# A gated-recurrence and soft-MoE kernel: the first k loaded as two transfers, and the transfer of u issued later

## The chip, the cores and the metric

The kernel runs on one core of one Trainium2 chip. The metric is the device time of one execution in microseconds (us); lower is better. A core has five engines that run their own instruction queues: TensorE (PE in the profile, its weight loads PEld), VectorE (DVE), ScalarE (ACT), GpSimd (POOL) and SyncE (SP, which here only issues DMA transfers). A transfer is spread over up to 16 DMA engines; each works through its part of the queue of transfers in order, and it is called a ring below.

## The reference, cut to what matters

There are two stages. The first is a linear recurrence over 768 steps for 4 batches and 8 heads with head size 48; `w` (decay) and `u` (bonus for the present step) hold one row of 48 per head. The second routes the 3072 resulting rows of width 384 through a soft mixture of 8 experts with 4 slots each.

```python
for t in range(S):                                  # r, k, v: (4, 8, 768, 48)
    cur = einsum('bhd,bhe->bhde', u[None] * k[:, :, t], v[:, :, t])
    y[:, :, t] = einsum('bhd,bhde->bhe', r[:, :, t], state + cur)
    state = w[None, :, :, None] * state + einsum('bhd,bhe->bhde', k[:, :, t], v[:, :, t])
x = y.transpose(0, 2, 1, 3).reshape(3072, 384)
logits = x @ phi                                    # (3072, 32)
d = softmax(logits, axis=0); slot_input = (d.T @ x).reshape(8, 4, 384)
for e in range(8):
    slot_out[e] = maximum(slot_input[e] @ w1[e], 0) @ w2[e]    # w1: 384x1024, w2: 1024x384
out = softmax(logits, axis=1) @ slot_out
```

## The kernel before, in words

The recurrence is done in chunks of 128 steps. Six chunks make a batch, and they are handled in 12 units of two chunks (three units a batch). `k`, `r` and `v` come in eight loads each, two per batch: load m is batch m // 2, its even m holds a third of the steps (384 KB, 128 partitions of 2 x 384 numbers), its odd m two thirds (768 KB). The middle dimension of 2 is the parity e of the head: partition p holds for some steps and a pair q of heads first the even head, then the odd one. `load_f` (lines 192 to 196) issues one such load as one transfer on SP.

A load is scaled by powers of w (`Sk`, `Sr`: line 427, a multiplication with a table `tabs` or `tabl`; `VC` is the plain copy of v, line 418), turned on TensorE (`Tk`, `Tr`, `Tv`: line 436) and copied out of PSUM (`Ek`, `Er`, `Ev`: line 359 on ACT, 357 on DVE). Then come the products in the chunk (`A`, line 506, masked by `K`, line 511), the state (`U`, `SM`, `SI`, `SE`), the result (`Y`) and, as results come in, the logits and the dispatch softmax of the second stage.

The expert weights, 16 matrices of 384 x 1024 numbers, are fetched by POOL and turned from f32 into bf16 on the way (`W0` to `W15`, lines 783 and 785). They go mostly into the same 14 buffers `raw` that the loads of k, r and v used. `W0` is issued behind a tiny copy (line 781) that waits for the seventh k. When the last weights are there, the last products (`Q12`, `Q13`, line 921) and one copy (line 928) give `slot_out`; then 24 tiles of the output are computed (line 949), copied out of PSUM (lines 951 and 953) and written by eight transfers on SP (line 955).

The order of nearly all work is written out by hand in the string `ORDER` (line 9). Each word is a task; tasks are emitted in that order, and so each engine's queue holds its own tasks in that order and works through them strictly. Words beginning with F are filler matmuls (line 861) that keep TensorE busy. An instruction waits only for what it reads, and for buffers.

Around the change the words are these. `Lk0`, `Lr0`, `Lv0` load the first k, r and v, `Lk1` and so on the next. `LU` (line 381) loads u, 4 partitions of 96 numbers, 1.5 KB. `CC` on DVE (line 383) runs `consts_c` (lines 290 to 293): a copy of a permutation out of PSUM and then two small copies, of w and of u, into two tiles `wu` (line 293). `CT` (lines 309 to 311) turns both on TensorE, `CA` on DVE copies the result (line 314), `CU` on POOL multiplies w and u into `ucol` (lines 317 and 318), and `CW` on ACT makes the decay `wT`. `ucol` is first read by `U0`. Ahead of all this the small table `w` is loaded by ACT (line 211).

Transfers that SP and ACT issue count on eight completion semaphores in turn, so the ninth of them waits until the first has landed, the tenth for the second, and so on. The order of issue is w, k0, r0, u, v0, k1, r1, v1, k2, r2, v2, k3, r3, v3, k4, ...: k2 waits for w, k3 for u, r3 for v0, v3 for k1, k4 for r1.

Of the kernel before, what the change touches and what calls it, by code (L numbers as in the profile page):

```python
# [6 lines left out]


ORDER = """
CB0 Lk0 Sk0 Lr0 Tk0 Sr0 LU Lv0 Ek0:ACT VC0:ACT Lk1 AHa AHb F0_2 Tr0 Lr1 PR0 TB0b F1_3 N0 TB0a F2_2 Tv0 Ev0 Lv1 CC Lk2  # L10
TB1b F3a_9 V0 CT Sk1b Sr1b Sk1a:DVE Lr2 Er0:ACT NE0:ACT CA F4a_11 Tk1b F5a_1 Tk1a VE0 A00 CB TB1a Ek1a VC1b VC1a:ACT
Lv2 CU K00 F6_4 Tr1b Tv1a Ek1b:ACT CW Ev1a Lk3 Sr1a F7y_1 U0 Er1b:ACT SM0 Sk2 N2 A01 K01 NE2:ACT Tv1b Sr2 Ev1b:ACT
Sk3a F8y_3 Tr1a SI0 Lr3 Lv3 N1 Sk3b Er1a:ACT Lk4 VC3b PR1b V1 A10 Sr3a DV0 VC2:ACT K10 Y0 NE1:ACT VE1:ACT Sr3b YE0 Tv2
# [32 lines left out]
class _Plan:  # L46
# [7 lines left out]
    def buf(self, pool):  # L54
        return _Buf(pool)

    def add(self, name, engs, fn, deps=(), bufs=()):
        self.by[name] = _Task(name, engs, fn, list(deps), list(bufs))
# [23 lines left out]
def kernel(  # L82
# [13 lines left out]
    B, H, S, D = r.shape  # L96
# [11 lines left out]
    R = 8  # L108
# [5 lines left out]
    CC = NS // U3  # L114
# [11 lines left out]
    def O(ins):  # L126
        return tc.keep_in_program_order(ins)

    pe, dve, act, pool, sp = nc.tensor, nc.vector, nc.scalar, nc.gpsimd, nc.sync
# [5 lines left out]
    RW = 2 * J * D  # L135
# [53 lines left out]

    def load_f(dst, a, m):
        b, lg = divmod(m, 2)
        jn = J if lg else JH
        O(sp.dma_start(out=dst[:, 0:2 * jn * D].rearrange("p (e x) -> p e x", e=2),  # L195
                       in_=a[b].rearrange("h (y j) d -> y h (j d)", j=jn)[lg * CC * R:lg * CC * R + 32]))

# [146 lines left out]
    def consts_d():  # L344
# [5 lines left out]
    L = _Plan(dict(raw=raw, ks=ks_t, vj=vj_t, kn=kn_t, vn=vn_t, AT=AT_t, prs=pr_t[0:1], prl=pr_t[1:2], dv=dv_t,  # L350
                   **{f"{x}T": t for x, t in turned.items()},
                   S=S_t, Z=Z_t, x=x_t, zc=zc_t, Lc=Lc_t, Lcl=[Lc_t[0][:, NS - 2:]], Lsl=[Ls_t[0][:, NS - 2:]], Ls=Ls_t, E=E_t, ET=ET_t, T=T_t, A=[Ab], Y=[Yb], M=[Mb], **{f"xT{j}": [t] for j, t in enumerate(xT_t)}))
    buf, add = L.buf, L.add
# [17 lines left out]
    for m in range(NLD):  # L371
        for i, nm in enumerate("krv"):

            b, o = (kr["k", m][0], RH) if nm == "r" and m % 2 == 0 else (buf("raw"), 0)
            kr[nm, m] = b, o
            add(f"L{nm}{m}", "SP", (lambda b, o, a, m: lambda t: load_f(b.inst[:, o:RW], a, m))(b, o, (k, r, v)[i], m), bufs=[b])

    def load_phi(t):
        O(sp.dma_start(out=phi_f, in_=moe_phi.rearrange("(p q) s -> p q s", q=nM)))
# [13 lines left out]
    for h, av_, x in (("a", argl, slice(0, JH + 1)), ("b", argm, slice(JH, J + 1))):  # L393
        add(f"AH{h}", "DVE", (lambda av_, x: lambda t: argv_part(av_, e17l[:, x]))(av_, x))
        for i in range(2):

            add(f"TB{i}{h}", "ACT", (lambda i, h, av_: lambda t: O(act.activation(  # L397
                out=tabl[i][:, :, JH:J] if h == "b" else tabl[i][:, :, 0:JH],
                in_=av_[:, :, 1 - i:JH + 1 - i], func=AF.Exp, scale=(-1.0, 1.0)[i])))(i, h, av_),
# [3 lines left out]
    for m in range(NLD):  # L403
        lg = m % 2
        pb = TT["p", m] = buf("pr" + "sl"[lg])
        for nm in "krv":
            dstT = TT[nm, m] = buf(nm + "sl"[lg] + "T")
            P = P2 if nm == "v" else 128
            for h in range(1 + lg):
# [11 lines left out]
                else:  # L421
                    i = "kr".index(nm)
# [42 lines left out]
    for n in range(NU):  # L465
# [4 lines left out]
        m = 2 * bt + (ui > 0)  # L470
# [50 lines left out]
        def f_su(t, Mf=Mf, kn=kn, vn=vn, Sold=Sold, pb=pb, n=n, NK=NK):  # L521
# [13 lines left out]
            bufs=[Mf, vn, pb_, kn] + ([Sold] if ui else []))  # L535
# [26 lines left out]
        def f_y(t, Yf=Yf, rT=rT, vn=vn, dvb=dvb, Sold=Sold, Smid=Smid, a=tuple(ATb), n=n):  # L562
# [18 lines left out]
            bufs=[Yf, rTb, vn, dvb, Smid, ATb[0], ATb[1]] + ([Sold] if ui else []))  # L581
# [213 lines left out]
    for n in range(2 * E):  # L795
        wat[n] = buf("raw")
        wat[n].left += 4
        bufs, deps = [wat[n]], []
# [6 lines left out]
    nm = nm_t[(NPC - 1) % 2]  # L805
# [14 lines left out]
        bufs=[SXb])  # L820
# [118 lines left out]
    i = 0  # L939
# [46 lines left out]
```

## Time and profile before

| what | us |
|---|---|
| median of 3 runs | 119.49 |
| their range | 119.38 to 120.67 |
| the profiled execution, its own time | 120.24 |
| its span in the trace | 118.5 |
| outside the span | 1.7 |
| busy: TensorE, weight loads | 98.0, 71.1 |
| busy: VectorE, ScalarE, GpSimd | 94.8, 86.6, 61.0 |

The span runs from the first to the last instruction that the trace shows; the rest of the execution's time lies around it. The page cuts the span into 40 slices of 2.96 us and prints one digit for each: 9 means busy for 90% or more. DMA is the mean busy share of the 16 rings. The chain of waits starts at the last instruction and follows back what released it. All moments below are us from the start of the span. The trace also records when each ring reports its part of a transfer as landed; a transfer has landed when its last ring has reported.

### The profile page before, as it was taken

The page shows a single profiled execution, that of the slowest core. Times are in us where ns is not written, and L with a number is a line of the kernel's source. Part 1 is how long each engine was busy: PE and PEld are TensorE (multiplying, and loading weights), DVE is VectorE, ACT ScalarE, POOL GpSimd, SP SyncE. Part 2 cuts the span into 40 slices and gives each one's busy share as a digit, 9 for nine tenths or more (in the row PEclk, how much of TensorE's full clock was granted, in tenths as well). Part 3 has the DMA queues.
Part 4 walks back from the last instruction along what each step waited for, and adds up shares of the span by engine and source line. Part 5 has one row for each costly group of instructions (what it writes and reads, how often), then busy time and mean ns, then how long its engine had stood idle before and what let it go on. Part 6 is the DMA issues. An engine that isn't in the chain of part 4 may idle for free.

```text
span 118.5 us, 3926 instructions
## 1 busy us (share of the span) xinstructions
PE 98.0 (83%) x1660; PEld 71.1 (60%) x1660; DVE 94.8 (80%) x180; ACT 86.6 (73%) x140; POOL 61.0 (52%) x79
## 2 busy tenths in 40 slices
PE   3997895999999999989999989999899985498000
PEld 0364674787888787867788878686453542254000
DVE  6899987898999999999999989999786274099100
ACT  5769894999999999989899799979644151269000
POOL 7605899999999989999999010002303000000000
PEclk9999999999999999999999999999999999869955
DMA  2999999999999999999999999999999995059994
GB/s 31 333 387 374 364 408 397 383 390 401 384 384 391 297 229 223 219 215 214 217 212 221 210 223 207 223 207 219 212 212 218 216 207 104 12 199 407 419 402 166
DMA packets 10441, 31.81 MB, mean 268 GB/s; under 512 B 1080, under 2 KB 4408, under 8 KB 10424
## 3 DMA queue, kind: packets, MB, share of 16 engines
q0 software_dynamic: 2448, 12.58, 51.8%
q1 hardware_dynamic: 7832, 18.93, 42.3%
q8 instruction: 13, 0.21, 0.7%
q10 hardware_dynamic: 144, 0.05, 0.2%
q14 instruction: 4, 0.03, 0.1%
HBM read 39.42 MB, written 4.72 MB: 373 GB/s over the span
## 4 chain that ended last, share of the span: by engine, by line
PE 32%; DMA 23%; POOL 15%; DVE 9%; ACT 6%; issue 4%; SPq 3%; DVEq 0%; ACTq 0%; POOLq 0%
DMA raw<-in_moe_w_dram 16%; POOL mix L427 12%; PE T L436 7%; DMA raw<-in_r_dram 7%; PE Ab L506 3%; DVE mix L953 2%; PE Yb L572 2%; SPq L195 2%; PE T L491 2%; PE Yb L567 2%; DVE AT_all L511 2%; ACT xT_all L359 2%; PE Yb L578 2%; PE T L481 2%; PE T L595 2%
## 5 line engine op out<-in xcount | busy, mean ns | idle before, releaser
L427 POOL TENSOR_TENSOR mix<-raw,tabl 128x768 bf16<-128x768 f32 x15 | 27.7, 1858 | 5.8 <-ACT tabl L397 5.4
L511 DVE TENSOR_TENSOR AT_all<-Ab,mask 128x1024 bf16<-128x1024 f32 x24 | 29.3, 1219 | 1.1 <-PE Ab L506 0.5
L359 ACT COPY mix<-T 128x1024 bf16<-128x1024 bf16 x19 | 19.1, 1021 | 3.9 <-PE T L436 2.3
L436 PEld LDWEIGHTS <-mix 128*128 128x128 bf16 x192 | 11.8, 99 | 2.3 <-DVE mix L427 0.7
L555 DVE TENSOR_TENSOR dv<-vn,Mb 128x768 bf16<-128x768 bf16 x12 | 11.4, 946 | 1.4 <-PE Mb L545 1.1
L427 POOL TENSOR_TENSOR mix<-raw,tabs 128x768 bf16<-128x768 f32 x6 | 10.8, 1815 | 0.0
L359 ACT COPY vT_all<-T 96x1024 bf16<-96x1024 bf16 x10 | 10.2, 1021 | 0.5 <-PE T L436 0.4
L506 PE MATMUL Ab<-mix 64*128 64x128 bf16 x192 | 9.5, 218 | 1.2 <-ACT mix L359 1.0
L359 ACT COPY xT_all<-T 128x768 bf16<-128x768 bf16 (+1 forms) x12 | 9.3, 784 | 1.3 <-PE T L595 1.3
L359 ACT CAST x<-Yb 128x768 bf16<-128x768 f32 x12 | 9.7, 808 | 0.0
L436 PE MATMUL T<-turnl,mix 128*128 128x128 bf16 x128 | 9.6, 219 | 0.1
L359 ACT COPY vn<-T 128x768 bf16<-128x768 bf16 x11 | 8.8, 814 | 0.0
L452 DVE TENSOR_TENSOR pr<-T,mix 128x1024 bf16<-128x1024 bf16 x12 | 8.0, 681 | 0.0
L712 POOL TENSOR_TENSOR Lc<-Ls,sm 128x192 bf16<-128x192 f32 x2 | 1.0, 516 | 13.5 <-ACT E L690 13.5
L506 PEld LDWEIGHTS <-mix 64*128 64x128 bf16 x192 | 5.8, 94 | 3.5 <-issue 0.7
L572 PEld LDWEIGHTS <-AT_all 128*128 128x128 bf16 x192 | 6.6, 96 | 1.6
L359 ACT COPY kn<-T 128x768 bf16<-128x768 bf16 (+1 forms) x10 | 7.2, 722 | 0.1
L418 POOL CAST vj<-raw 128x768 bf16<-128x768 f32 x8 | 6.7, 832 | 0.6 <-POOL phi_s L336 0.6
L436 PEld LDWEIGHTS <-vj 128*96 128x96 bf16 x96 | 6.2, 123 | 1.2 <-issue 0.2
L572 PE MATMUL Yb<-vn,AT_all 128*128 128x48 bf16 x192 | 6.8, 183 | 0.0
L539 DVE TENSOR_TENSOR Z<-Mb,wT 128x384 bf16<-128x384 f32 x12 | 6.6, 553 | 0.1
L481 PE MATMUL T<-ident,mix 128*128 128x128 bf16 x80 | 6.1, 219 | 0.2
(187 smaller groups left out, 237.8 us busy)
## 6 DMA issues: line engine op xcount, KB each, us to landing
raw<-in_moe_w_dram POOLq DMA_DIRECT2D x13, 768.0 KB, 14.4
raw<-in_k_dram SPq DMA_DIRECT2D x4, 768.0 KB, 12.2
raw<-in_r_dram SPq DMA_DIRECT2D x4, 768.0 KB, 12.2
raw<-in_v_dram SPq DMA_DIRECT2D x4, 768.0 KB, 12.2
out_dram<-mix SPq DMA_DIRECT2D x3, 768.0 KB, 4.6
raw<-in_k_dram SPq DMA_DIRECT2D x4, 384.0 KB, 10.9
raw<-in_r_dram SPq DMA_DIRECT2D x4, 384.0 KB, 10.6
raw<-in_v_dram SPq DMA_DIRECT2D x4, 384.0 KB, 10.8
```

Source lines behind the costliest of these rows:

```text
L195: O(sp.dma_start(out=dst[:, 0:2 * jn * D].rearrange("p (e x) -> p e x", e=2), in_=a[b].rearrange("h (y j) d -> y h (j d)", j=jn)[lg * CC * ...
L359: O(act.copy(dst, src))
L418: O(act.copy(o, i_) if t.eng == "ACT" else pool.tensor_copy(o, i_))
L427: O(eng.tensor_mul(src.inst.rearrange("p (j e s) -> p e j s", j=JH, e=2)[:, :, :, 0:D], rv(), tab))
L436: O(pe.transpose(Tb.inst[0:P, jj * 128:(jj + 1) * 128], sv[:, jj, :], (turn, turnl)[lg][:]))
L452: O(dve.tensor_mul(cv(pb), tv(), cv(kT)))
L481: O(pe.transpose(Tb.inst[:, x * 128:(x + 1) * 128], kT.inst[:, x, :], ident[:]))
L506: O(pe.matmul(Abf.inst[:, e, x * C:(x + 1) * C], kT.inst[s, g * nQ + x, :], rT.inst[s, g * nQ + x, :]))
L511: O(dve.tensor_mul(AT.inst[:], Abf.inst[:].rearrange("p e (g t) -> p e g t", g=nQ), mask[:, None, None, :].to_broadcast([128, 2, nQ, C])))
L539: O(dve.tensor_mul(Smid.inst[:], Mf.inst[:, 0:SW].rearrange("p (q d) -> p q d", q=nQ)[:, :, None, :].to_broadcast([128, nQ, 2, D]), wT[:, ...
L555: O(dve.tensor_mul(dvb.inst[:].rearrange("p g e d -> p (g e) d"), vn.inst[:].rearrange("p g e d -> p (g e) d"), Mf.inst[:, 448:448 + 2 * P ...
L572: O(pe.matmul(y[:, x // nQ, q * P2 + e * D:q * P2 + (e + 1) * D], a[x // nQ].inst[:, e, q, :], vn.inst[:, x, e, :], start=False, stop=(c = ...
```

## The change

The first k is loaded by two transfers, one for the even heads and one for the odd heads, 192 KB each, with the same rows of 1536 bytes. `LU` moves in `ORDER` from its place ahead of `Lv0` to the place behind `Lv1`. All else stays in its order on every engine: on SP the queue becomes k0 even, k0 odd, r0, v0, k1, r1, v1, u, k2, ... Among the eight semaphores the order is now w, k0 even, k0 odd, r0, v0, k1, r1, v1, u, k2, ...: u waits for w, k2 and r2 for the halves of k0, v2 for r0, k3 for v0, r3 for k1, v3 for r1, k4 for v1, r4 for u. `Sk0` waits for both halves.

```diff
 ORDER = """
-CB0 Lk0 Sk0 Lr0 Tk0 Sr0 LU Lv0 Ek0:ACT VC0:ACT Lk1 AHa AHb F0_2 Tr0 Lr1 PR0 TB0b F1_3 N0 TB0a F2_2 Tv0 Ev0 Lv1 CC Lk2
+CB0 Lk0 Sk0 Lr0 Tk0 Sr0 Lv0 Ek0:ACT VC0:ACT Lk1 AHa AHb F0_2 Tr0 Lr1 PR0 TB0b F1_3 N0 TB0a F2_2 Tv0 Ev0 Lv1 LU CC Lk2
...
-    def load_f(dst, a, m):
+    def load_f(dst, a, m, halves=False):
         b, lg = divmod(m, 2)
         jn = J if lg else JH
+        if halves:
+            for e in range(2):
+                O(sp.dma_start(out=dst[:, e * jn * D:(e + 1) * jn * D],
+                               in_=a[b].rearrange("(q e) (y j) d -> e y q (j d)", e=2, j=jn)[e, lg * CC * R:lg * CC * R + 32]))
+            return
         O(sp.dma_start(out=dst[:, 0:2 * jn * D].rearrange("p (e x) -> p e x", e=2),
                        in_=a[b].rearrange("h (y j) d -> y h (j d)", j=jn)[lg * CC * R:lg * CC * R + 32]))
...
-            add(f"L{nm}{m}", "SP", (lambda b, o, a, m: lambda t: load_f(b.inst[:, o:RW], a, m))(b, o, (k, r, v)[i], m), bufs=[b])
+            add(f"L{nm}{m}", "SP", (lambda b, o, a, m, hv: lambda t: load_f(b.inst[:, o:RW], a, m, hv))(b, o, (k, r, v)[i], m, m == 0 and i == 0), bufs=[b])
```

## The prediction

> **What bounds the kernel now.** I read the page's slices first, then the chain of waits, then the stretches and the start in order of time.
>
> ```profile
> span 118.5 us, 3926 instructions
> PEclk9999999999999999999999999999999999869955
> DMA  2999999999999999999999999999999995059994
> ...
> 82.73 18.82 DMA raw<-in_moe_w_dram
> 101.60 0.51 PE Yb L921 x7
> ```
>
> The rings are full from the second slice to the 33rd, then nearly idle for two slices, then full with the output. The chain ends in the last weights, which were issued at 82.73 but landed only at 101.56, because the rings were still working off earlier transfers. So the time is: the rings' start (first packet of k0 at 2.42), their fixed work without a hole, and a tail behind the last weights. In the trace the busy share of the rings stays within a few per cent of full between 3.1 and 97, and the largest dip, between r0 and v0 (4.8 to 5.6), adds up to some 0.1 us. A transfer of weights comes nearest to being late at W7, issued at 60.54, when the first ring runs out of W6 at 64.72: 4.2 us to spare. The engines have slack against this, seen in the next view (busy us of each engine in a stretch, last the granted TensorE clock, DMA share, GB/s).
>
> ```profile
> 10.44:13.85 3.41, 2.29 (x22) 1.35 (x20) 3.30 (x8) 3.41 (x5) 3.07 (x2) 1.00 0.99 353
> 13.85:17.27 3.42, 3.42 (x70) 2.77 (x68) 3.08 (x6) 2.93 (x7) 3.27 (x5) 1.00 1.06 404
> 17.27:20.68 3.41, 2.13 (x36) 1.67 (x34) 2.43 (x4) 1.93 (x3) 3.41 (x3) 1.00 1.03 399
> ...
> 99.20:102.60 3.40, 1.05 (x16) 0.27 (x8) 0.00 (x0) 0.13 (x1) 0.00 (x0) 1.00 0.21 36
> 102.60:106.00 3.40, 3.00 (x11) 1.77 (x11) 2.28 (x5) 2.11 (x5) 0.00 (x0) 0.50 0.32 118
> ```
>
> Between 17.27 and 20.68 PE idles 1.28 and DVE about 1.0, waiting for POOL. Before the last weights PE waits 2.17 (row at 101.60 of the timeline). A lateness of DVE or PE under about 2 us is gone by then. The start, in order of time:
>
> ```profile
> 0.73 0.71 SPq L195 DMA_DIRECT2D raw<-in_k_dram  x1
> 1.49 0.80 SPq L195 DMA_DIRECT2D raw<-in_r_dram  x1
> 2.35 0.53 SPq L381 DMA_DIRECT2D LexpT<-in_u_dram  x1
> 2.91 0.60 SPq L195 DMA_DIRECT2D raw<-in_v_dram  x1
> ...
> 10.68 1.65 DVE L293 COPY wu<-LexpT 4x96 f32<-4x96 f32 x2
> 12.25 0.94 DVE L427 TENSOR_TENSOR mix<-raw,tabl 128x768 bf16<-128x768 f32 x1
> ...
> 12.26 0.34 PE L311 MATMUL Yb<-ident_f,wu 4*128 4x4 f32 x2 [1.12 <-DVE wu L293]
> ```
>
> SP spends 0.5 to 0.8 us on each issue, whatever its size. DVE reaches the copy of u at about 12.1, and PE already waits 1.12 for it.
>
> **The change part by part.**
>
> *k0 in halves.* One issue of 0.71 becomes two. The nearest rows for a half: the first output transfer, also 128 rows of 1536 bytes, took 0.36 to issue, and w on ACT, 128 rows, 0.63. So the second half is issued at 1.1 to 1.4 and done at 1.5 to 2.0. k0's first packet came 0.98 after its issue ended (1.44 to 2.42), so the first half's could come 0.1 to 0.35 sooner. But w's packets share the rings from 2.16 on, and k0's first packets took up to 0.7 us each against 0.065 later; that start-up would not shrink. I take 0.15 sooner; ends 0 and 0.35. The bytes, rows and packets are the same, so the rest of the rings' work keeps its length. k0 as a whole landed at 4.86; DVE began `Sk0` at 5.46, right behind the table that ACT finished at 5.43. So a sooner k0 speeds no engine, and it may be 0.57 later at no cost; after that, DVE's start is late by the same amount. One more semaphore to wait on at `Sk0`: under 0.05, beside ACT's 0.83 on the other table.
>
> *r0* is issued up to 0.6 later (at most 2.0 to 2.8). With k0's 0.98 its packets come at 3.8 at the latest; the fastest ring finished k0 at 3.79, the slowest after 4.4. A hole of 0.0, at most 0.6 if an issue is as slow as r0's 0.80; I take 0. v0, k1, r1 and v1 have one issue more (the half) and one less (u) ahead: 0.3 sooner to 0.1 later. I take 0.05 for the dip at 4.8 to 5.6, where u stood between r0 and v0; ends 0 and 0.1.
>
> *u behind v1.* SP issues u at about 5.6 instead of 2.35, and k2 and all behind it up to 0.6 later: the rings hold k1, r1 and v1 then, until 12.2 at least. The shift in semaphores delays k3, r3, v3 and k4: v3 (issued at 11.30) now waits for r1, landed 12.35, and k4 (12.37) for v1, landed 14.31. The first ring needs k4's packets only at 21.2, when it is done with v3: covered by 6 us. Cost 0.
>
> u itself now lies behind v1 on its rings. Before, it was reported at 5.46 to 5.58 on four rings, amid r0's reports (5.16 to 5.83); the other twelve reports came at once, at 3.00. Now it follows v1, whose rings reported from 12.22 to 14.31, median 12.8. I take 12.9; ends 12.3 and 14.4. The Trainium skill (DMA: Bandwidth & Descriptors, "Why a DMA increments its semaphore by 16") says that a transfer of 4 rows runs on the four lowest engines and that the rest is counted at once; the four late reports agree, but no row says whether the slow ring is among the four.
>
> DVE's copy of u then ends at about 13.0 instead of 12.33. Queued behind it on DVE: `Sk1a`, `CA`, `VE0`, the clearing of Mb, all 0.7 late (0 to 2.1). PE stands at `CT`, and behind it F4a, `Tk1b`, `Tk1a`, the first A. ACT waits for `Tk1b`. POOL wants `wuT` at 15.60 only, and it was there at 13.27: 2.3 to spare. POOL is not late, and PE and DVE regain the 0.7 between 17.27 and 20.68, where they wait for POOL's products. Cost 0 at the end; without that cover 0.7, and 2.17 of waiting before the last weights would still swallow it.
>
> *Sum*: 120.24 of the profiled execution - 0.15 - 0.05 = 120.04. That execution was 0.75 above the median of 119.49, so I forecast **119.3**.
>
> **The rivals.**
>
> *A, the forecast*: rings start slightly sooner, engines hidden: 119.3 (bounds -0.45 to +0: 119.0 to 119.5).
>
> *B, slower: PE falls to half clock behind the late u.* In the stretch before 102.60, PE was busy 1.05 of 3.40, and the next stretch was granted 0.50. With 2.29 and 2.13 of 3.41 the clock stayed. If u lands at 13.5 or later, the stretch 10.44 to 13.85 keeps only about 0.9 (0.51 at 10.63 and the last 0.3). Then 13.85 to 17.27, where PE is full, does half its work: 1.7 late, beside up to 2.1 from the wait. It decides if more than 2.17 of these 3.8 is still there at 99.4: 119.5 + 3.8 - 2.17 = 121.1. For it: PE and DVE are over 95% busy from 30 to 78, and regain little there. Against: the idle 1.28 at 17.3 to 20.7 alone makes it 119.8, and u must be late. The Trainium skill (TensorE: Matmul & The Clock Gate, the rules at its end) puts the limit at idle gaps above about 3 us; by that, a gap from 11.14 to 12.9 costs no clock, and the time would be A's. The trace speaks against so wide a limit: the half clock at 102.60 followed a wait of 2.17.
>
> *C, a hole in the rings behind k0's second half*: r0 comes 0.6 after the rings ran dry, 119.5 + 0.6 - 0.15 = 119.9. Against: the 3.8 and 3.79 above.
>
> *D, faster: the tail keeps its clock.* The output's first matmuls, nine from 103.00 to 105.73, take 2.73 at clock 0.50; at full clock half, 1.36. If the wait before the last weights falls so that no stretch is mostly idle, up to 1.2 of that is saved: 119.3 - 1.2 = 118.1. For it: a shift of the rings' end moves that wait. Against: 0.2 is little, and the copies behind the matmuls (0.49 each on two engines) hide part.
>
> *E, no sooner start*: the start-up packets set the pace, and the halves gain nothing: 119.5. The Trainium skill (DMA: Bandwidth & Descriptors, "Rules for kernel authors") says of two transfers to disjoint partition halves not to bother, since they share the same engines; here it is halves of each row, but by that rule E holds.
>
> **How the numbers follow.** A 0.40, E 0.22, C 0.08, B 0.18, D 0.12. A measurement of this kernel can tell about 1%, 1.2 us, from no change. A, C and E lie within it: same 0.70; B gives slower 0.18, D faster 0.12. The range leaves out half of B and of D with some of the noise of the runs' 1.3: 118.4 to 120.9. The likeliest case's own range is 119.0 to 119.7.
>
> **What would show it.** Two k0 rows on SP of 0.36 to 0.63 each, and v0 issued by 3.0: else the first part is wrong. `Sk0` starting at 5.4 to 5.6. The second copy of L293 ending near 13.0, with PE's wait at L311 near 1.8. POOL's L427 still at 10.3 and 12.5, its ucol near 15.6. Rings full from 3 to 97, last weights at 101.2 to 101.6, a wait of about 2 before them. Wrong would be: a granted 0.50 early on, a PE without a wait before the last weights, a hole in the rings at 3.8.

## The result and the profile after

The changed kernel takes 120.55 us (median of 22 runs, 119.53 to 121.82) beside 119.36 us for the kernel before in the same series (22 runs). The ratio is 1.008, with a 95% interval of 1.0054 to 1.0106: slower, by about 1 us. The profiled execution took 121.15 us with a span of 119.4.

Ratios and intervals here and below leave out runs more than 1.5% above the fastest of their kernel, which takes out six of the twelve runs of e13 (the mean of all twelve is 1.0% above the kernel before) and at most a quarter of the runs of any other variant.

The page of the changed kernel, its slices first. (Lines of the code are six later than before: L427 is L433, L293 is L299, L311 is L317, L921 is L927.)

```profile
span 119.4 us, 3927 instructions
PEclk9999958999999999999999999999999999999965
...
PE 49%; DVE 21%; DMA 7%; issue 5%; ACT 4%; SPq 4%; POOL 2%; DVEq 1%; ACTq 0%
```

Three things are new. The clock is down in the sixth and seventh slice. It is no longer down at the start of the output (before: 8 and 6 in the 35th and 36th). And the chain that ended last holds only 7% of DMA, all of it waiting for u, against 23% before: it ends in PE, not in the last weights. The same stretches as in the prediction (busy us of PE, weight loads, DVE, ACT, POOL; clock; DMA share; GB/s):

```profile
10.44:13.85 3.41, 1.62 (x14) 0.76 (x12) 2.70 (x4) 3.41 (x5) 2.58 (x2) 1.00 1.03 409
13.85:17.27 3.42, 2.31 (x7) 0.89 (x8) 2.54 (x7) 1.86 (x3) 3.27 (x5) 0.69 1.06 386
17.27:20.68 3.41, 3.41 (x44) 2.83 (x43) 1.43 (x2) 1.71 (x5) 1.51 (x1) 0.81 1.03 401
99.20:102.60 3.40, 2.83 (x48) 1.79 (x45) 2.79 (x10) 1.26 (x4) 0.00 (x0) 1.00 0.50 90
102.60:106.00 3.40, 2.79 (x30) 1.82 (x28) 1.69 (x5) 2.00 (x6) 0.00 (x0) 1.00 0.02 5
```

PE did 1.62 us of work between 10.44 and 13.85 where it had done 2.29, and 7 operations in the next stretch where it had done 70. The half clock lies between 15.16 and 18.58. Between 17.27 and 20.68 PE no longer waits for POOL: it is full, and the others wait for it. Between 99.20 and 102.60 PE is busy for 2.83 where it had been for 1.05.

The timeline of the start, SP first, then DVE and PE:

```profile
0.73 1.36 SPq L198 DMA_DIRECT2D raw<-in_k_dram  x2
2.15 0.62 SPq L201 DMA_DIRECT2D raw<-in_r_dram  x1
...
5.68 1.03 SPq L387 DMA_DIRECT2D LexpT<-in_u_dram  x1
```

```profile
5.51 0.96 DVE L433 TENSOR_TENSOR mix<-raw,tabs 128x768 bf16<-128x768 f32 x1
7.28 0.96 DVE L433 TENSOR_TENSOR mix<-raw,tabs 128x768 bf16<-128x768 f32 x1 [0.81 <-DMA raw<-in_r_dram]
...
11.62 1.52 DVE L299 COPY wu<-LexpT 4x96 f32<-4x96 f32 x1
14.61 0.30 DVE L299 COPY wu<-LexpT 4x96 f32<-4x96 f32 x1 [1.46 <-DMA LexpT<-in_u_dram]
```

```profile
14.96 0.22 PE L317 MATMUL Yb<-ident_f,wu 4*128 4x4 f32 x1 [1.54 <-DVE wu L299]
15.11 2.52 PE L867 MATMUL Ab<-mix,ident 128*128 128x512 bf16 x6
...
19.08 0.40 PE L512 MATMUL Ab<-mix 64*128 64x128 bf16 x8
...
101.32 0.83 PE L927 MATMUL Yb<-raw,AT_all 128*32 128x384 bf16 x16 [0.52 <-DVE AT_all L363]
...
103.38 0.50 PE L927 MATMUL Yb<-raw,AT_all 128*32 128x384 bf16 x8
```

The rows of PE before that belong beside them:

```profile
12.53 1.36 PE L861 MATMUL Ab<-mix,ident 128*128 128x512 bf16 x6
...
14.83 0.40 PE L506 MATMUL Ab<-mix 64*128 64x128 bf16 x8
...
101.60 0.84 PE L921 MATMUL Yb<-raw,AT_all 128*32 128x384 bf16 x8 [2.17 <-DMA raw<-in_moe_w_dram]
```

r0 is issued at 2.15 instead of 1.49 and DVE now waits 0.81 for it. u lands only at 14.6, and DVE waits 1.46 for it. PE waits for DVE, and the six filler matmuls behind that wait take 2.52 at the lower clock instead of 1.36. At the end the products of the last weights (103.38) start with no wait at all, where before there was one of 2.17. How the lateness runs through the two traces:

| moment | before | after | later by |
|---|---|---|---|
| DVE starts the first copy into `wu` | 10.68 | 11.62 | 0.94 |
| PE starts the filler behind `CT` | 12.53 | 15.11 | 2.58 |
| PE ends that filler | 13.89 | 17.63 | 3.74 |
| PE starts the first products `A` | 14.83 | 19.08 | 4.25 |
| POOL runs the gate of `W0` | 35.42 | 38.61 | 3.19 |
| PE could start on the last weights (before: 101.60 - 2.17) | 99.43 | 103.38 | 3.95 |
| PE starts on them | 101.60 | 103.38 | 1.78 |
| end of the span | 118.46 | 119.35 | 0.89 |

So in these two executions u holds PE until it is 2.58 late. The 0.94 by which DVE was late because of r0 is no part of a sum here: an earlier DVE would only have waited longer for u. The half clock adds 1.67 by 19.08, where PE has had work without a break. Of these 4.25, PE regains 1.08 by about 22, where it had waited 1.28 for POOL before. Between 47 and 70 it loses 0.97 again, and no run here asks why. Of the 3.95 that are left at the last weights, the former wait swallows 2.17. An output that runs at full clock (0.33 instead of 0.52 for a matmul of 384 columns) goes with 0.89 less behind it.

The rings show the late r0, and more in their bytes than in their busy share. The stretches in which r0 and what follows are fetched, before and then after:

```profile
3.40:4.60 1.20, 1.20 (x5) 0.50 (x4) 0.97 (x3) 0.53 (x3) 1.20 (x3) 1.00 1.02 371
4.60:6.00 1.40, 1.40 (x4) 0.44 (x3) 1.27 (x5) 1.40 (x3) 0.35 (x3) 1.00 1.01 327
6.00:10.00 4.00, 3.88 (x40) 2.53 (x39) 4.00 (x8) 2.65 (x5) 0.00 (x0) 1.00 1.03 389
```

```profile
3.40:4.60 1.20, 1.20 (x5) 0.51 (x4) 0.81 (x2) 0.53 (x3) 1.20 (x3) 1.00 0.93 243
4.60:6.00 1.40, 1.40 (x4) 0.46 (x3) 1.25 (x5) 1.40 (x3) 0.34 (x3) 1.00 0.87 264
6.00:10.00 4.00, 3.70 (x35) 2.37 (x34) 3.19 (x6) 2.11 (x4) 0.00 (x0) 1.00 0.97 315
```

The share falls by a tenth, the bytes by a third (371 to 243 GB/s) and stay a fifth lower until 10. A packet counts as busy as long as it takes, and from 3.6 to 5.3 fourteen packets of 1536 bytes took 0.31 to 1.16 us, where the median of such packets is 0.065 (before, six took 0.35 to 0.53 from 4.0 to 5.8). That these are the first packets behind a pause is likely but not shown: the trace does not tell which ring a packet ran on. By 10 us 2.13 MB of k, r, v and u had come instead of 2.61.

### The profile page after: what moved, and what is told of

Read it like the earlier page. It is cut to its first block, busy times and chain, and to the rows that moved or that the text cites. A ratio compares the mean times of both kernels' runs of the same rounds, so it can differ in the third digit from the quotient of the medians.

```text
span 119.4 us, 3927 instructions
## 1 busy us (share of the span) xinstructions
PE 99.6 (83%) x1660; PEld 72.1 (60%) x1660; DVE 94.4 (79%) x180; ACT 87.0 (73%) x140; POOL 61.3 (51%) x79
## 4 chain that ended last, share of the span: by engine, by line
PE 49%; DVE 21%; DMA 7%; issue 5%; ACT 4%; SPq 4%; POOL 2%; DVEq 1%; ACTq 0%
PE T L442 11%; DMA LexpT<-in_u_dram 7%; DVE AT_all L517 5%; PE Ab L512 4%; DVE mix L959 3%; PE Yb L578 3%; PE Ab L867 3%; SPq L201 3%; PE Yb L927 3%; PE Yb L573 3%; PE Yb L584 2%; PE T L487 2%; PE T L601 2%; PE T L497 2%; PE Mb L535 2%
## 5 line engine op out<-in xcount | busy, mean ns | idle before, releaser
L433 POOL TENSOR_TENSOR mix<-raw,tabl 128x768 bf16<-128x768 f32 x15 | 27.1, 1818 | 6.4 <-ACT tabl L403 6.3
L442 PEld LDWEIGHTS <-mix 128*128 128x128 bf16 x192 | 12.3, 102 | 3.3 <-DVE mix L433 1.7
L433 POOL TENSOR_TENSOR mix<-raw,tabs 128x768 bf16<-128x768 f32 x6 | 10.8, 1820 | 2.3 <-PE Yb L867 2.3
L442 PE MATMUL T<-turnl,mix 128*128 128x128 bf16 x128 | 10.1, 226 | 0.1
L424 POOL CAST vj<-raw 128x768 bf16<-128x768 f32 x8 | 7.5, 935 | 0.6 <-POOL phi_s L342 0.6
L867 PE MATMUL Ab<-mix,ident 128*128 128x512 bf16 (+1 forms) x23 | 7.1, 409 | 0.0
```

Source lines behind the costliest of these rows:

```text
L424: O(act.copy(o, i_) if t.eng == "ACT" else pool.tensor_copy(o, i_))
L433: O(eng.tensor_mul(src.inst.rearrange("p (j e s) -> p e j s", j=JH, e=2)[:, :, :, 0:D], rv(), tab))
L442: O(pe.transpose(Tb.inst[0:P, jj * 128:(jj + 1) * 128], sv[:, jj, :], (turn, turnl)[lg][:]))
L867: O(pe.matmul(o[:, 0:256 * min(n, 2)], ident[:], mix[:, 0:256 * min(n, 2)], start=True, stop=True))
```

## The experiments

Two theories were to be told apart. **U**: the late u makes DVE and PE wait, PE's clock is halved, and the end becomes PE's. **H**: one more issue on SP ahead of r0 leaves the rings dry near 4 us, and all transfers are late. The last column counts the executions whose mean granted clock was below 0.95; one more half stretch of 3.41 in 119 lowers the mean by 0.014. It does not catch every early half stretch: the profiled execution of the kernel before, with its half stretch at the output, has a mean of 0.962, and that of the whole change, with an early one and none there, 0.964.

| kernel | median us, runs | ratio to the kernel before, 95% interval | clock < 0.95 |
|---|---|---|---|
| the whole change | 120.55, 22 | 1.008 [1.0054, 1.0106] | 9 of 22 |
| e16, the whole change again | 120.97, 6 | 1.0107 [1.0057, 1.0158] | 3 of 6 |
| e1, halves only | 120.84, 6 | 1.011 [1.006, 1.016] | 0 of 6 |
| e13, halves only again | 121.18, 12 | 1.0033 [0.9988, 1.0079] | 0 of 12 |
| e2, late u only | 120.78, 12 | 1.0065 [1.0026, 1.0105] | 1 of 12 |
| e14, late u only, filler ahead of `CT` | 120.54, 12 | 1.0057 [1.0019, 1.0095] | 1 of 12 |
| e9, whole change, filler ahead of `CT` | 120.01, 12 | 0.9994 [0.9954, 1.0035] | 0 of 12 |
| e3, whole change, u used later | 119.9, 12 | 1.0024 [0.9992, 1.0057] | 0 of 12 |
| e4, before, u used later | 119.26, 12 | 0.9982 [0.9946, 1.0018] | 0 of 12 |
| e8, before, u behind k1 | 120.45, 12 | 1.0009 [0.996, 1.0059] | 1 of 12 |
| e11, before, u behind k2 | 120.97, 12 | 1.009 [1.0056, 1.0125] | 5 of 12 |
| e15, halves, u behind k1 | 120.22, 12 | 1.003 [0.9991, 1.0069] | 0 of 12 |
| e5, halves, u on POOL's queue | 120.3, 12 | 1.0031 [0.9985, 1.0077] | 0 of 12 |
| e6, before, u on POOL's queue | 119.87, 12 | 0.9978 [0.9936, 1.002] | 0 of 12 |
| e7, before, u ahead of r0 | 120.44, 12 | 1.0025 [0.9978, 1.0072] | 0 of 12 |
| e12, before, u ahead of k0 | 119.52, 12 | 0.9983 [0.9945, 1.0022] | 0 of 12 |
| e10, before, u on POOL's queue and used later | 119.79, 12 | 1.0026 [0.9992, 1.006] | 0 of 12 |

The kernel before had a clock below 0.95 in 3 of the 128 runs beside them. Medians of different chips aren't compared: the kernel before had 119.37 beside e1 to e4, 120.28 beside e5 to e8, 120.01 beside e9 to e12, 119.58 beside e13 to e16.

### Each part by itself: e1, e2, e13

Fragments of the first line of `ORDER`; e1 and e13 are the changed kernel with u put back, e2 is the kernel before with u moved:

```diff
 # e1, e13 against the changed kernel
-Sr0 Lv0 Ek0:ACT
+Sr0 LU Lv0 Ek0:ACT
-Tv0 Ev0 Lv1 LU CC Lk2
+Tv0 Ev0 Lv1 CC Lk2
 # e2 against the kernel before
-Sr0 LU Lv0 Ek0:ACT
+Sr0 Lv0 Ek0:ACT
-Tv0 Ev0 Lv1 CC Lk2
+Tv0 Ev0 Lv1 LU CC Lk2
```

> The first k in halves, u in its old place behind r0. Theory 1 (the late u holds DVE and PE, and the halves cost nothing that lasts): as the kernel before, 119.4, ratio 0.998 to 1.002; the second copy of wu ends near 12.3 and PE's clock stays at 1.00. Theory 2 (the later r0 leaves the rings empty at 4 to 5, and everything behind comes later): the whole loss, about 120.3, ratio 1.006 to 1.010, with r0 landing near 7 instead of 5.8.

> The first k whole, u issued behind the third v. Theory 1: the whole loss, 120.3, ratio 1.006 to 1.010; the copy of u waits until 14.3 or later, PE is granted less than full clock in the stretch behind it. Theory 2: as the kernel before, 119.4, r0 landing at 5.8.

> The first k in halves alone, u in its old place, once more, beside the whole change on the same chip. Read as two causes that each cost (two issues ahead of v0 leave the rings dry; the late u slows PE), this should lie at 0.3 to 0.7% over the kernel before and below the whole change. If the 1.1% of its first measurement is real, it lies at or above the whole change, and the halves are the main cause.

Late u alone loses 0.65%. Its trace shows the same picture as the whole change: a half clock from 14.98 to 18.40, and no wait before the last weights. Its rows of DVE, POOL and PE:

```profile
11.32 1.53 DVE L293 COPY wu<-LexpT 4x96 f32<-4x96 f32 x1
13.44 1.34 DVE L293 COPY wu<-LexpT 4x96 f32<-4x96 f32 x1 [0.59 <-DMA LexpT<-in_u_dram]
...
10.97 3.75 POOL L427 TENSOR_TENSOR mix<-raw,tabl 128x768 bf16<-128x768 f32 x2 [6.03 <-DMA raw<-in_k_dram]
```

```profile
14.84 0.22 PE L311 MATMUL Yb<-ident_f,wu 4*128 4x4 f32 x1 [1.72 <-DVE wu L293]
14.99 2.53 PE L861 MATMUL Ab<-mix,ident 128*128 128x512 bf16 x6
...
102.78 0.63 PE L921 MATMUL Yb<-raw,AT_all 128*32 128x384 bf16 x8
```

Here u landed at 13.42, DVE had waited for it no more than 0.59, and still the copy ended only at 14.79. POOL was at work on its multiplications until 14.72. So PE (14.84) came nearly as late as in the changed kernel (14.96), without a late r0 and with u 1.16 sooner. A copy that falls into a multiplication of POOL's ends with it, in the other traces too (see the end).

The halves alone were measured at 1.1% in six runs, which was as much as the whole change, and at 0.33% in the repetition. The two intervals overlap only from 0.6 to 0.79%, so the size of this loss is open. In none of 18 executions was the mean clock below 0.95, and in both traces the end is still the rings'. But e13's trace has an early half clock as well, from 21.45 to 24.86, and PE comes to the last weights 2.2 late. r0 did not land near 7 here, as e1's second theory has it, but at 5.64 (e1) and 6.09 (e13); the second k was late, at 11.11 and 11.55 instead of 9.45. In e13's timeline, on SP:

```profile
2.71 0.53 SPq L387 DMA_DIRECT2D LexpT<-in_u_dram  x1
3.29 0.61 SPq L201 DMA_DIRECT2D raw<-in_v_dram  x1
```

In its stretches, to be read against the two tables above:

```profile
3.40:4.60 1.20, 1.20 (x5) 0.50 (x4) 0.56 (x2) 0.40 (x2) 1.20 (x3) 1.00 0.88 260
4.60:6.00 1.40, 1.40 (x4) 0.44 (x3) 1.25 (x6) 1.32 (x3) 0.34 (x3) 1.00 0.88 251
6.00:10.00 4.00, 3.83 (x36) 2.40 (x35) 4.00 (x7) 2.66 (x5) 0.00 (x0) 1.00 0.90 292
```

And on PE, behind the last weights:

```profile
102.86 0.79 PE L927 MATMUL Yb<-raw,AT_all 128*32 128x384 bf16 x8 [1.20 <-DMA raw<-in_moe_w_dram]
```

With u in its old place v0 has one issue more ahead of it than in the kernel before (it is issued at 3.29 instead of 2.91), and the rings bring less than in any other kernel here: 2.10 MB by 10 us. The last weights' products start 1.26 later than before, still behind a wait for the transfer.

### u late, but nothing waits for it: e3, and the control e4

`CC`, `CT` and `CA` move behind the work that had stood behind them; e4 is the same on the kernel before:

```diff
-Ev0 Lv1 LU CC Lk2
-TB1b F3a_9 V0 CT Sk1b Sr1b Sk1a:DVE Lr2 Er0:ACT NE0:ACT CA F4a_11 Tk1b F5a_1 Tk1a VE0 A00 CB TB1a
+Ev0 Lv1 LU Lk2
+TB1b F3a_9 V0 Sk1b Sr1b Sk1a:DVE Lr2 Er0:ACT NE0:ACT F4a_11 Tk1b F5a_1 Tk1a VE0 CB CC CT A00 CA TB1a
```

> The changed kernel, with the copies of u on DVE, their turn on TensorE and the copy behind it moved later in the order (behind VE0, Tk1a and the clearing of Mb), so that little stands behind the wait for u. Theory 1: the loss goes, 119.4 (ratio 0.998 to 1.003), PE busy over 2 of 3.41 from 10.44 on and the clock kept. Theory 2: still 120.3, since the rings' hole at the start is still there.

> The kernel before with that same later use of u, as the control for it. Both theories: no change within 0.3%, 119.1 to 119.7; if it is faster, the place of the copies cost something before as well (DVE spent 1.65 in them beside POOL's multiplication).

The slices and PE's rows of e3:

```profile
PEclk9999999999999999999999999999999999999855
```

```profile
15.82 0.22 PE L317 MATMUL Yb<-ident_f,wu 4*128 4x4 f32 x1 [0.79 <-DVE wu L299]
...
101.97 0.78 PE L927 MATMUL Yb<-raw,AT_all 128*32 128x384 bf16 x8 [1.22 <-DMA raw<-in_moe_w_dram]
```

In e3 the early half clock is gone and a wait of 1.22 for the last weights is back, with u and the halves where the change puts them. 0.24% of loss is left, against 0.8 to 1.07%. So most of what the whole change loses hangs on waiting for u. Against its control (0.9982) e3 would still lose 0.42%; both intervals hold 1.

### How late is too late: e8, e11, e12

```diff
-Sr0 LU Lv0 Ek0:ACT VC0:ACT Lk1 AHa
+Sr0 Lv0 Ek0:ACT VC0:ACT Lk1 LU AHa          # e8
-Ev0 Lv1 CC Lk2
+Ev0 Lv1 Lk2 LU CC                           # e11
-CB0 Lk0 Sk0 Lr0
+CB0 LU Lk0 Sk0 Lr0                          # e12
```

> The kernel before with u issued behind k1: v0 and k1 come 0.57 sooner, u lands with k1, near 9.5, ahead of the 12.1 at which DVE wants it. If the late u loses through DVE's and PE's wait alone: 119.4 or less, PE's clock at 1.00. If taking u away from between r0 and v0 hurts the rings by itself: 120 or more, with a dip at 5 to 6.

> The first k whole, u one place later still than in the changed kernel, behind the fourth k: u lands with k2, near 15.6 instead of 14.5. If the late u's wait is what costs: ratio 1.010 to 1.016, more than the 1.0065 of u behind v1, DVE's copy of u ending about 1 us later. If the cost does not grow with the wait: 1.005 to 1.008.

> The kernel before with u issued ahead of the first k: k0 and r0 come 0.57 later, v0 and the rest as before, no ring goes dry in between. It prices a late start of the rings. If the end goes with the rings: 0.3 to 0.6 us longer, ratio 1.002 to 1.005. If the engines' slack hides it: 1.000.

Behind k1 u is there when DVE comes to it, and no loss can be told from noise (1.0009). Behind v1 0.65% is lost (e2), behind k2 0.9%, which lies between the two ranges expected. Two rows of e8, of DVE and PE:

```profile
11.66 1.64 DVE L293 COPY wu<-LexpT 4x96 f32<-4x96 f32 x2
...
101.41 0.82 PE L921 MATMUL Yb<-raw,AT_all 128*32 128x384 bf16 x8 [1.00 <-DMA raw<-in_moe_w_dram]
```

e8 is the best control for the whole change. DVE comes to these copies at 11.66, as late as there (11.62), but finds u. PE stays 0.98 late from then on to the last weights, where the wait shrinks from 2.17 to 1.00 and nothing of it is left. So about 1 us of lateness costs nothing here that can be told from noise, as the prediction said; what costs is the wait for u on top. The dip that e8's expectation names did come: the rings brought 264 GB/s between 4.6 and 6.0 instead of 327.

e11's two rows, of DVE and PE:

```profile
15.59 0.20 DVE L293 COPY wu<-LexpT 4x96 f32<-4x96 f32 x1 [3.10 <-DMA LexpT<-in_u_dram]
...
16.04 2.53 PE L861 MATMUL Ab<-mix,ident 128*128 128x512 bf16 x6
```

The wait for u grew from 0.59 (e2, also with k0 whole) to 3.10, its PE doesn't wait for the last weights either, and 5 of 12 executions have the low clock. u ahead of everything, which starts k0 later, costs nothing that can be measured.

### PE kept at work while it would wait: e9, e14

```diff
-TB1b F3a_9 V0 CT Sk1b Sr1b Sk1a:DVE Lr2 Er0:ACT NE0:ACT CA F4a_11 Tk1b
+TB1b F3a_9 V0 F4a_11 CT Sk1b Sr1b Sk1a:DVE Lr2 Er0:ACT NE0:ACT CA Tk1b
```

e9 is the changed kernel with this, e14 is e2 with it.

> The changed kernel with the six filler matmuls F4a moved on TensorE from behind the turn of u to ahead of it: DVE waits for u as long as in the changed kernel, but PE works 1.4 of that time and should keep its clock in the stretch behind. If the half clock makes most of the late u's loss: back to ratio 1.002 to 1.004. If the wait in the queues makes it: still 1.006 to 1.008, with the clock at 1.00.

> k0 whole, u behind the third v, and the filler F4a_11 ahead of CT, so that PE works while it would wait for u. If the loss of the late u alone (0.65%) is the half clock behind an idle PE, this is within 0.2% of the kernel before and its mean clock is that of the kernel before; if it is the waiting queues of DVE and PE, about 0.5% of loss stays.

The six filler matmuls now run before the wait. The low clocks are nearly gone (1 of 24, against 12 of 28 for the whole change), but the mean over the runs, 0.960 (e9) and 0.961 (e14), is still below the 0.966 and 0.967 of the kernel before beside them. e9 lost nothing that can be told from noise, e14 lost 0.57%. The intervals overlap, and how much a late u costs by the queues alone is not shown. The trace of e9 shows that the cure isn't certain. PE still waits 1.70 for DVE's copy of u, and the clock is halved from 16.48 to 19.90:

```profile
PEclk9999976999999999999999999999999999999855
```

### One issue more ahead of r0: e5, e7, e15, with e6 and e10

```diff
-    add("LU", "SP", lambda t: O(sp.dma_start(...)))
+    add("LU", "POOL", lambda t: O(pool.dma_start(...)))   # e5 (halves), e6 and e10 (k0 whole)
-CB0 Lk0 Sk0 Lr0 Tk0 Sr0 LU Lv0
+CB0 Lk0 Sk0 LU Lr0 Tk0 Sr0 Lv0                           # e7 (k0 whole)
-Sr0 LU Lv0 Ek0:ACT VC0:ACT Lk1 AHa
+Sr0 Lv0 Ek0:ACT VC0:ACT Lk1 LU AHa                       # e15 (halves)
```

e10 has u on POOL's queue and the later use of e4.

> The first k in halves, u issued by POOL (idle from 5 to 10 in the kernel before) instead of SP, so that v0 and all behind it are issued on SP as early as before and only r0 0.6 later; u lands before DVE wants it. Theory H (a load that SP issues too late leaves rings dry, and dry rings restart with packets of 0.3 to 1.7 us): rings dip near 4, about half of the loss of the halves alone, 119.7 to 120.2. Theory S (only the late u costs, and the halves alone lost by something else than SP's time): 119.4 or less.

> The first k whole and u issued by POOL: SP has one issue fewer than before, v0 and all behind it come 0.57 sooner. Theory H: no dip at 5, 119.0 to 119.4, as fast as the kernel before or faster. Theory S: 119.4.

> The kernel before with u issued between k0 and r0: no halves, no late u, only one more issue ahead of r0, and v0 as before. Theory H: rings dry near 4 as with the halves, 119.8 to 120.3. If the loss came from the halves themselves (w's small packets pushed back, shorter transfers), this is 119.4.

> The first k in halves, u issued behind the second k: one issue more ahead of r0 and of v0, none more ahead of what follows, and u in time for DVE. If the whole change loses by its late u, this is within 0.3% of the kernel before; if the late r0 behind the second half is the cause, it loses 0.7% or more like the whole change.

> The kernel before with both mild gains so far together: u issued by POOL (ratio 0.9978 alone) and used later (0.9982 alone). If both are real and add up: 0.994 to 0.998, 118.8 to 119.2. If each was chance: 1.000.

e5 and e15 have the halves and a u in time, e7 has a whole k0 with the tiny u issued between k0 and r0: 1.0031, 1.003, 1.0025. Each interval takes in 1, so a loss of about 0.3% is not shown, though the three agree with each other and with e3 over e4. What they share is one issue more ahead of r0, and with it a hole in the rings: in all nine such traces they brought 243 to 294 GB/s between 3.4 and 4.6, in the nine others 320 to 383. e7 shows that the issue need not be a half of k0:

```profile
3.40:4.60 1.20, 1.20 (x5) 0.51 (x4) 0.97 (x3) 0.53 (x3) 1.20 (x3) 1.00 0.84 243
4.60:6.00 1.40, 1.40 (x4) 0.44 (x3) 1.27 (x5) 1.40 (x3) 0.35 (x3) 1.00 0.90 300
6.00:10.00 4.00, 4.00 (x32) 2.68 (x31) 3.63 (x7) 2.20 (x5) 0.00 (x0) 1.00 1.00 353
```

Two things speak against reading the hole as the cause of a loss. Rings that are late at the start are not special to these kernels: k1 landed by 9.64 at the latest in the kernel before, e4 and e6, and at 10.47 to 11.55 in all fifteen other traces, e8 and e12 among them, which lose nothing measurable. And at the end the products of the last weights started at 102.43 (e7) and 102.48 (e15) instead of 101.60, but at 101.46 in e5. So theory H is right about the hole; that it costs time is not shown.

Taking u off SP gives nothing that can be told from noise (e6), and together with the later use (e10) it gives nothing either, so no version here beats the kernel before.

### The whole change once more: e16

> The changed kernel again, as the measure for the three beside it: 0.5 to 1.1% over the kernel before by every theory, mean clock of its executions some 0.01 lower.

Its trace holds two half stretches in a row, from 13.44 to 20.27, where the first profile held one:

```profile
10.44:13.85 3.41, 1.34 (x12) 0.66 (x11) 2.48 (x4) 3.41 (x5) 2.80 (x2) 0.94 1.04 409
13.85:17.27 3.42, 1.76 (x5) 0.76 (x6) 2.45 (x5) 1.64 (x3) 2.12 (x5) 0.50 1.06 385
17.27:20.68 3.41, 3.41 (x29) 2.50 (x28) 0.95 (x4) 1.45 (x4) 1.64 (x1) 0.56 1.03 401
```

With the first 22 runs that makes 28 executions of the changed kernel. None has a mean clock between 0.946 and 0.952: 12 with 0.941 to 0.946 take 121.35 us in the mean, 16 with 0.952 to 0.975 take 120.21. All runs of the kernel before beside them have a mean of 119.6 and 119.8. So of the 1.0 us that the change costs in the mean, about half (12 / 28 x 1.13 = 0.49) goes with the lowest clocks. That is no measure of all that the half clock costs: the first profiled execution, with an early half stretch, is among the 16.

## Why the prediction was wrong, point by point

The range of 118.4 to 120.9 holds the 120.55, and the loss is about the 1% named as the measure. But the forecast was 0.2 us faster, and the time is 1.2 slower by a mechanism that the prediction had as rival B with 0.18. Rival C's hole in the rings (0.08) came as well, but what it costs is not shown.

*k0 in halves.* Nearly right in the rows named: two issues of 0.64 and 0.67 (at most 0.63 was said), `Sk0` at 5.51 (5.4 to 5.6 was said). Both halves had landed by 4.42 instead of 4.86, and it sped no engine, as said. v0 was issued at 2.81, by 3.0 as said. The 0.15 of a sooner start did not come in the profiled pair: k0's first packet ran at 2.41, before at 2.42 (in six other traces it was 0.26 to 0.29 sooner, see the end).

*r0: "I take 0"* failed. r0 was issued 0.66 later and its end came 1.35 later (7.18 instead of 5.83). The working compared the moment of r0's packets (3.8) with the moment when the fastest ring was done with a k0 that starts as before. But the halves ended sooner, too: the rings reported the second one from 4.05 to 4.42, and k0 before from 4.16 to 4.86. And r0's packets did not go on at 0.065 each (see the end). DVE, which does `Sr0` in order, started it about 0.9 late. The upper bound of 0.6 was too low.

*The dip where u stood, 0.05 to gain*, went the other way. With k0 whole and u no longer between r0 and v0, v0 was issued 0.39 to 0.58 sooner and yet landed at 8.57 to 9.26 in six of seven traces (e2, e8, e10, e11, e12, e14; not e6), against 7.49 before and 7.19 in e4. Why is open.

*"Cost 0" of the late u* is the step that failed most. Three things in it were too small. First, u was taken to land at 12.9, by the median of v1's rings; it landed at 14.58, with v1's rings at 13.24 to 14.55. A transfer has landed when its last ring has, and u comes behind v1 on its rings: here the bound of 14.4, by the slowest of them, was the near one (in e2, e3, e9, e14 and e16, with the same place for u, it was 13.42 to 14.69). Second, the copy itself was put at 0.1 ("ends at about 13.0"). In the kernel before, the copies took 1.65 beside POOL, and PE's wait of 1.12 was for the first of them, that of w. POOL's second multiplication ran until 14.85 in the changed kernel and until 14.72 in e2, and the copy ended at 14.91 and 14.79: so even a u at 13.42 was of little use. Third, no half clock was reckoned: what stands behind the wait was "0.7 late (0 to 2.1)", and it was 2.58 late, and 4.25 by the first `A`. That PE regains time by 22, where it had waited for POOL, was right, by 1.08; but the lateness was larger than that and the 2.17 together. POOL now waits 2.32 for PE instead of PE 1.28 for POOL.

```profile
16.43 0.20 POOL L323 TENSOR_TENSOR ucol<-wuT 64x4 bf16<-64x4 f32 x1
...
21.10 1.82 POOL L433 TENSOR_TENSOR mix<-raw,tabs 128x768 bf16<-128x768 f32 x1 [2.32 <-PE Yb L867]
```

"POOL is not late" failed as well: its first multiplication starts at 11.27 instead of 10.33, behind a table that came late, and `ucol` comes at 16.43, 0.83 late.

*Rival B* was the right mechanism. It priced 3.8 late at the front, less 2.17: 1.6. In the profiled pair it was 3.95, less 2.17, less 0.89. Its 1.7 for the half clock was met by 1.67, its condition that u be late was met, and its "regain little there" (30 to 78) was right: nothing was regained. What it lacked is that with a PE that ends last the output keeps its clock: rival D's mechanism came with rival B and took half of its price away. D had 1.2 for it, 0.89 was seen.

*The clock.* The prediction set the Trainium skill's rule (TensorE: Matmul & The Clock Gate, the rules at its end: no idle gaps above about 3 us) against the half clock behind a wait of 2.17, and judged the rule too wide. The runs bear that out: gaps of 1.54 and 1.72, each with a shorter one ahead of it, were enough. The unit is not the gap. Cut each of the 18 traces into stretches of 3.41 that end where a half clock begins. Behind the first 5 us, each of the 15 stretches in which PE was busy for some time but for 1.59 or less was followed by the half clock, among them 0.74 (the changed kernel, 11.75 to 15.16), 0.58 (e2) and 0.22 (e11). None with 2.13 or more was. In between it went both ways: 7 of 16, with 1.72 (e9), 1.75 (e10) and 2.12 (e12) among the 7, and 1.67 (e5), 1.74 (e7) and 1.82 (e14) among the others. These stretches begin at another moment in each execution (the half clock at 15.16 and at 13.44 in two of the same kernel), so the same idle time sometimes falls into one and sometimes is split over two. That could make the low and the higher mean clocks of the 28 executions, but only two of them have a trace (one half stretch at a mean of 0.964, two at 0.941), so it is not shown. The Trainium skill says in Part 1 of the same page that the clock is decided in windows of 3413 ns that run freely; the stretches of 3.41 with a varying start agree.

*Rival E and the Trainium skill's rule* (DMA: Bandwidth & Descriptors, "Rules for kernel authors": don't bother with two transfers to disjoint partition halves) pointed the right way: the halves gained nothing. Neither names a cost. With u in time the split was measured at 0.3% (e5, e15: 1.0031 and 1.003), and each interval takes in 1.

*What stays open.* The halves with u in its old place were measured at 1.1% (e1) and 0.33% (e13); the lower bytes at the start are shown, but not why half of e13's runs are 121.5 to 122.3 and half 119.4 to 120.9. So it is open, too, whether the parts add up to the 0.8 to 1.07% of the whole. And e9 against e14 (0.9994, 1.0057) leaves open how much of a late u's loss is the clock's.

## What to carry to other kernels

A small transfer that is put behind large ones on the same rings can land as late as the slowest ring of the last of them, so reckon with the latest landing, with what the engine that uses it shares with another engine at that moment, and with every engine whose in-order queue stands behind the one that waits. A wait early on that leaves PE busy for less than half of 3.4 us costs twice, once as a wait and once as a half clock; here PE was 4.25 late at 19 us and 4.14 late at the end of the weights, over busy engines. Before an issue is added ahead of a kernel's first loads, see whether the rings have data to bridge its 0.6 us: a hole shows in GB/s more than in the busy share. Whether it costs anything depends on the slack behind it, so price the slack first.

## What the runs showed of the hardware

- Where rings stood dry (9 to 15 packets under way from 4.0 to 5.0 in the changed kernel, 15 to 19 before), packets took longer and counted as busy meanwhile: r0's and v0's 0.31 to 1.16 us instead of a median of 0.065, four of k1's 1.04 to 1.72 instead of 0.121. The busy share was 0.93 at 243 GB/s, against 1.02 at 371.
- An issue on SP took about 0.6 us whatever it moved: 0.61 for 768 KB (the changed kernel's k1), 0.64 for 192 KB, 0.53 for the 1.5 KB of u (e13). Single rows of the first 5 us lie between 0.37 (u, e12) and 1.10 (v1, e8).
- A copy of 4 x 96 f32 numbers on DVE that began more than 0.1 us into a multiplication of POOL's ended 0.06 or 0.07 us behind it: 13.14 and 14.91 behind 13.08 and 14.85 (the changed kernel), 14.79 behind 14.72 (e2), 14.61 behind 14.55 (e14), 14.74 behind 14.68 (e9). With POOL idle it took 0.19 or 0.20 (e13, e11).
- In e1, e3, e5, e9, e13 and e16 the first half of k0 began 0.26 to 0.29 sooner (2.13 to 2.16) and got among the small packets of w: w landed at 3.70 to 3.87, instead of 3.41 before, and ACT's first table came 0.3 to 0.45 later. e3 and e5 lose no more than e15, where w landed as before.
